# A planned attention and mixer kernel on one core: the set-up reordered, one more transpose and mixer buffer, a new plan

## The chip, the cores and the metric

The kernel runs on one core of a Trainium2 chip. The metric is the device time of one execution in microseconds. Five engines work side by side, each through its own queue in order: PE (matrix multiply), DVE (VectorE), ACT (ScalarE), POOL (GpSimd) and SP, which here only issues transfers. An instruction that waits for a semaphore holds back everything behind it on its engine.

## The reference, cut to what matters

The sequence has 2048 tokens (16 tiles of 128) of width D = 448, all in bf16. Two layers run one after the other with the same weights, each an attention block (16 heads of 28) and a mixer block:

```
_A_ref(x, wqkv, wo):  qkv = x @ wqkv;  p = softmax(q k^T / sqrt(28));  return (p v) @ wo
_B_ref(x, w1, w2, w3, w4):
    h  = gelu(layernorm(x) @ w1)
    hs = (four quarters of h, shifted by -1, +1, -2, +2 tokens) @ w2
    x1 = x + hs
    return x1 + gelu(layernorm(x1) @ w3) @ w4

x = x + _A_ref(layernorm(x), A_wqkv, A_wo)
x = x + _B_ref(layernorm(x), B_w1, B_w2, B_w3, B_w4)
(both lines once more)
```

The softmax needs some bound on each row of scores. The kernel takes a bias from norms: for each head the largest squared norm of a key, scaled by the square root of a ratio between the key weights and the query weights. That ratio only shifts the scores; the softmax does not depend on its exact value.

## The kernel before, in words

**Attention.** The heads are stored in groups of 32 columns, so that four groups `g` of four heads fill 128 partitions. The scores are formed as key tile by query chunk: a *block* is one key tile (128 keys) of one head against one query chunk of 512 (or two key tiles against a chunk of 256). ACT takes the exponential of blocks in PSUM (line 1367), three blocks in one instruction (128x1536) and two in the next (128x1024), and writes them to `PT`. PE then multiplies `PT` with the values `vaug` (line 736); column 28 of each head in `vaug` is 1.0, so that the sum of the exponentials comes out with the values. A few blocks do not go to ACT: DVE computes their exponential by a polynomial into buffers `PD` (lines 1253, 1274, 1276, 1278, 1281). There are 1024 blocks in each layer.

**Order of the blocks.** `ORDER` lists segments (query chunk, first and last key tile), each for g = 0 to 3. Layer 0 begins with query chunk 0 against key tiles 0 to 3 (64 blocks), then tiles 4 to 7 (blocks 64 to 127), then 8 to 15 (from block 128), and only then goes on to query chunk 1. Layer 1 begins with query chunk 0 against key tiles 0 to 6 (112 blocks), then query chunk 1 against the same tiles. A segment that carries on an earlier one first needs the norm bound over all its key tiles, and adds the difference to the stored queries (`t_qp`, line 1234).

**Projections.** A layer norm writes a tile to `xn`; it is transposed to `xT` (two buffers of 512 tokens), by PE for the first chunk and by a transposing transfer afterwards. From `xT` PE forms keys, values and queries (line 745, `wk_pad`, `wv`, `wq_pad`). ACT or POOL squares keys and queries; PE sums the squares per head with `astat` (keys) or `astatq` (queries), and DVE takes the largest (`kmaxc`, line 1036). A transposed buffer is held from its load until every projection from it is done.

**Set-up.** DVE and POOL write constants and pads, among them the pad columns of `vaug` (POOL, lines 804 and 805). The query and key weights are packed to 32 columns per head (lines 828 to 833). The ratio comes from the squares of all 448 weight rows (line 839), summed by PE (line 841 holds the DVE form of the square), with a square root on POOL (line 854). It goes into `RTN` (line 856), which scales the key bound, and into `astatq` (line 860), which scales the summed squares of the query. The first query chunk adds that sum into its own PSUM bank (line 1067) before it is copied out (line 1060 or 1058).

**Who decides the order.** All work is written as small tasks that yield operations with an assumed duration. When the kernel is built, a planner (`Sched`) takes the tasks in order of priority (`RANK`, `Q_LEAD`), assigns buffers and PSUM banks, and writes down one fixed order for each engine. While PE would idle, it inserts *fillers*, small matmuls on `ident` (line 1783) whose result is never read. `D_RATE` and `DPK` say how many blocks DVE may take. `DOUBT` adds time to what PE waits for when the planner compares candidates. On the chip each engine simply follows its list.

**Mixer.** `t_mixA` normalises, transposes and multiplies with `w1`; `t_mixB` does the shifted multiply with `w2` into a buffer `x1b` (two of them), normalises, transposes, and multiplies with `w3` and `w4`. It runs beside the exponentials of the next query chunks; for the last chunk of layer 1 it forms the tail of the kernel. The GELU of a group is one long ACT instruction with a table load before and after it.

Of the kernel before, what the change touches and what calls it, by code (L numbers as in the profile page):

```python
# [515 lines left out]
DPK = 1  # L516
RANK = {k: round(1.1 + 0.05 * i, 3) for i, k in enumerate([('a', 0, 0), ('k', 0, 1), ('b', 0, 0), ('b', 0, 1), ('k', 1, 0), ('k', 0, 2), ('q', 0, 1), ('k', 0, 3), ('k', 1, 1), ('k', 1, 2), ('a', 0, 1), ('q', 0, 2), ('q', 0, 3), ('a', 0, 2), ('q', 1, 0), ('q', 1, 1), ('b', 0, 3), ('b', 0, 2), ('a', 0, 3), ('a', 0, 4), ('k', 1, 3), ('b', 0, 4), ('k', 1, 4), ('b', 1, 0), ('a', 1, 3), ('a', 1, 0), ('q', 1, 3), ('a', 1, 4), ('a', 1, 2), ('a', 1, 1), ('b', 1, 4), ('q', 1, 2), ('b', 1, 3), ('b', 1, 2), ('b', 1, 1)])}
Q_LEAD = {(0, 1): 4, (0, 2): 10, (0, 3): 3, (1, 0): 9, (1, 1): 8, (1, 2): 4, (1, 3): 3}
D_RATE = {(0, 0): 0.08, (0, 1): 0.05, (0, 2): 0.05, (0, 3): 0.13, (1, 0): 0.16, (1, 1): 0.1, (1, 2): 0.16}
# [10 lines left out]
Sched.DOUBT = {"dma": 1.0, "pool": 0.4, "dve": 0.05, "act": 0.2}  # L530
# [14 lines left out]
def build_kernel(nc, A_x, A_wqkv, A_wo, B_x, B_w1, B_w2, B_w3, B_w4, out, n_layers=2):  # L545
    S = A_x.shape[1]
    D = 448
# [19 lines left out]
    NPD = 6  # L567
# [56 lines left out]
    with st:  # L624
# [15 lines left out]
        halfs = sb("halfs", [128, 4], FP32)  # L640
        neghalf = sb("neghalf", [128, 4], FP32)
# [7 lines left out]
        x1b = sb("x1b", [128, 2, D], FP32)  # L649
# [42 lines left out]
        RTN, TMP, T2 = (sc[:, i, :] for i in range(3))  # L692
# [7 lines left out]
        xst = h2T[:, :, :].rearrange("p a b -> p (a b)").rearrange("p (t d) -> p t d", d=D)  # L700

# [56 lines left out]
        def t_load():  # L758
# [3 lines left out]
            def xload(a, b, t):  # L762
                return dma("sp", lambda e: e.dma_start(out=xst[:, a:b, :], in_=xin[:, a:b, :]), writes=[(("xst",), i) for i in range(a, b)], t=t)

            yield xload(0, 1, 3.0)
            yield xload(1, 2, 3.1)
            yield xload(2, 3, 3.2)
            yield xload(3, 4, 3.3)
            for ci, d3 in ((1, wst[1]), (0, wst[0])):
                yield dma("sp", lambda e, d3=d3, ci=ci: e.dma_start(out=d3[:, 0:3, :], in_=A_wqkv[0:384, ci * D:(ci + 1) * D].rearrange("(c p) n -> p c n", p=128)),  # L770
                          writes=[("pt", 4 * ci + k) for k in range(3)], t=4.6 + 1.4 * (1 - ci))
                yield dma("sp", lambda e, d3=d3, ci=ci: e.dma_start(out=d3[0:64, 3, :], in_=A_wqkv[384:448, ci * D:(ci + 1) * D]),
                          writes=[("pt", 4 * ci + 3)], t=4.6 + 1.4 * (1 - ci))
            yield dma("sp", lambda e: e.dma_start(out=wv[:, 0:3, :], in_=A_wqkv[0:384, 2 * D:3 * D].rearrange("(c p) n -> p c n", p=128)), writes=[(("wv",), 0)], t=6.0)
            yield dma("sp", lambda e: e.dma_start(out=wv[0:64, 3, :], in_=A_wqkv[384:448, 2 * D:3 * D]), writes=[(("wv",), 1)], t=6.0)
            yield xload(4, 8, 8.0)
            yield ("wait", ("start",))
            yield xload(8, 12, 8.0)
            yield xload(12, 16, 9.0)
# [12 lines left out]
        def t_setup():  # L792
            wst = [PT[:, 0:4, 0:D], PT[:, 4:8, 0:D]]
            wsq = PT[:, 8:12, :]
            yield op("dve", 0.1, lambda e: e.memset(ones_f[:, :], 1.0), writes=[("ones_f",)])
            yield op("dve", 0.1, lambda e: e.memset(ones_bf[:, :], 1.0), writes=[("ones_bf",)])
            yield op("pool", 0.5, lambda e: e.affine_select(out=ident[:, :], in_=ones_bf[:, :], pattern=[[-1, 128]],
# [6 lines left out]
            yield op("pool", 1.3, lambda e: e.memset(vaug[:, :, :].rearrange("p t (h r) -> p t h r", r=32)[:, :, :, 28:32], 0.0), writes=[("vaug_all",)])  # L804
# [1075 lines left out]
```

## Time and profile before

| | us |
|---|---|
| three runs | 1082.04, 1082.95, 1082.1 (median 1082.1) |
| the profiled execution, its own time | 1080.76 |
| the profiled execution, span from the first to the last instruction | 1079.0 |
| busy: PE / ACT / DVE / POOL | 1009.5 / 1016.7 / 642.3 / 315.8 |
| first exponential starts | 21.83 |
| last exponential ends | 1024.65 |
| granted TensorE clock | 0.994 |

A line of the profile's groups names line, engine, operation, output and input with their shapes, the count, busy time and mean duration, and then the idle time just before these instructions and what ended most of it. In the timeline the columns are start, length, engine, line and operation; what stands in brackets is the idle time before it and the instruction that released it. The profiled execution took 1.34 us less than the median of the runs, and 1.76 us of it lie outside the span.

### The profile page before, as it was taken

The page shows a single profiled execution, that of the slowest core. Times are in us where ns is not written, and L with a number is a line of the kernel's source. Part 1 is how long each engine was busy: PE and PEld are TensorE (multiplying, and loading weights), DVE is VectorE, ACT ScalarE, POOL GpSimd, SP SyncE. Part 2 cuts the span into 40 slices and gives each one's busy share as a digit, 9 for nine tenths or more (in the row PEclk, how much of TensorE's full clock was granted, in tenths as well). Part 3 has the DMA queues.
Part 4 walks back from the last instruction along what each step waited for, and adds up shares of the span by engine and source line. Part 5 has one row for each costly group of instructions (what it writes and reads, how often), then busy time and mean ns, then how long its engine had stood idle before and what let it go on. Part 6 is the DMA issues. An engine that isn't in the chain of part 4 may idle for free.

```text
span 1079.0 us, 35560 instructions
## 1 busy us (share of the span) xinstructions
PE 1009.5 (94%) x16117; PEld 426.2 (39%) x16117; DVE 642.3 (60%) x1250; ACT 1016.7 (94%) x922; POOL 315.8 (29%) x503
## 2 busy tenths in 40 slices
PE   6999899999989999999999999999899999999998
PEld 3333343443333244333333334353333343444465
DVE  8766678846588525675446652524685685564451
ACT  5999899999999999999998999999999999999952
POOL 3244126302264014453212210102624230432140
PEclk9999999999999999999999999999999999999999
DMA  4438211003121013211121222423321110121000
GB/s 134 118 97 233 69 57 32 21 19 91 32 31 32 12 57 79 49 31 27 35 85 41 44 79 92 137 58 99 61 42 36 38 45 13 32 65 30 2 20 33
DMA packets 92615, 62.27 MB, mean 58 GB/s; under 512 B 64688, under 2 KB 82368, under 8 KB 92464
## 3 DMA queue, kind: packets, MB, share of 16 engines
q1 hardware_dynamic: 89088, 51.92, 18.9%
q0 software_dynamic: 3376, 8.09, 2.7%
q8 instruction: 126, 2.06, 0.8%
q14 instruction: 25, 0.20, 0.1%
HBM read 27.12 MB, written 15.71 MB: 40 GB/s over the span
## 4 chain that ended last, share of the span: by engine, by line
ACT 72%; PE 18%; DVE 6%; DMA 3%; issue 1%; POOL 1%; SPq 0%; DVEq 0%; ACTq 0%
ACT PT L1367 65%; PE ps L745 9%; PE ps L1212 4%; PE ps L736 4%; ACT h2T L1742 3%; ACT fb L1616 1%; DMA rT<-ub 1%; PE ps L1783 1%; ACT L1742 1%; DMA xT<-xn 1%; ACT L1367 1%; DVE st L876 1%; DMA fb<-rscr 0%; DVE rT L1461 0%; DVE hT L1596 0%
## 5 line engine op out<-in xcount | busy, mean ns | idle before, releaser
L1367 ACT ACTIVATE PT<-ps 128x1536 bf16<-128x1536 f32 (+1 forms) x803 | 918.8, 1338 | 17.6 <-PE ps L1212 16.8
L1212 PE MATMUL ps<-qT,kT 32*128 32x512 bf16 (+1 forms) x2560 | 314.7, 341 | 35.4 <-ACT PT L1367 26.7
L736 PE MATMUL ps<-PT,vaug 128*32 128x512 bf16 (+1 forms) x2520 | 250.7, 341 | 0.2 <-DVE ub L1446 0.2
L1212 PEld LDWEIGHTS ps<-qT,kT 32*128 32x128 bf16 x2560 | 80.5, 91 | 310.1 <-ACT PT L1367 279.5
L1783 PE MATMUL ps<-ident 128*32 128x256 bf16 x3860 | 173.4, 278 | 6.0 <-DVE qT L1084 2.2
L745 PE MATMUL ps<-xT,w 128*32 128x512 bf16 (+2 forms) x2176 | 165.0, 362 | 5.3 <-DMA xT<-xn 3.2
L1783 PEld LDWEIGHTS ps<-ident 128*32 128x32 bf16 x3860 | 110.7, 97 | 38.0 <-issue 13.2
L1733 DVE CAST h2T<-ps 128x512 bf16<-128x512 f32 (+2 forms) x109 | 65.7, 603 | 79.0 <-PE ps L745 70.1
L736 PEld LDWEIGHTS ps<-PT,vaug 128*32 128x32 bf16 x2520 | 74.8, 95 | 92.8 <-issue 79.3
L745 PE MATMUL ps<-w,h2T 128*32 128x448 bf16 x1512 | 100.7, 357 | 9.0 <-ACT h2T L1742 9.0
L1472 POOL TENSOR_TENSOR otn<-ub,fb 128x512 bf16<-128x512 f32 (+1 forms) x36 | 42.1, 1169 | 150.8 <-DMA fb<-rscr 150.5
L745 PEld LDWEIGHTS ps<-xT,w 128*32 128x32 bf16 (+1 forms) x2176 | 59.6, 96 | 55.5 <-issue 29.3
L1011 POOL TENSOR_TENSOR sq<-kT 128x512 bf16<-128x512 bf16 (+2 forms) x32 | 30.2, 947 | 122.7 <-DVE kT L1025 122.6
L1614 POOL TENSOR_TENSOR fb<-hT 112x512 f32<-112x512 bf16 (+1 forms) x36 | 38.6, 1074 | 71.6 <-DVE hT L1596 54.7
L745 PEld LDWEIGHTS ps<-w,h2T 128*32 128x32 bf16 x1512 | 40.7, 96 | 43.1 <-issue 14.6
L1688 POOL TENSOR_TENSOR x_res<-x_res,x1b 128x448 f32<-128x448 f32 x32 | 40.1, 1257 | 35.8 <-DVE xn L896 30.8
L745 PE MATMUL ps<-xT,wk_pad 128*32 128x512 bf16 (+2 forms) x576 | 48.8, 359 | 0.4 <-DVE qT L1058 0.4
L1461 DVE RECIPROCAL rT<-rT 16x128 f32<-16x128 f32 (+1 forms) x36 | 33.6, 934 | 22.2 <-DMA rT<-ub 22.1
L1253 DVE TENSOR_SCALAR yd<-ps 128x512 int32<-128x512 f32 x40 | 27.2, 685 | 31.4 <-PE ps L1212 30.8
L1011 POOL TENSOR_TENSOR sq<-qT 128x512 bf16<-128x512 bf16 x28 | 29.6, 1065 | 49.0 <-DVE qT L1058 44.7
L745 PE MATMUL ps<-xT,wq_pad 128*32 128x512 bf16 x512 | 42.8, 382 | 0.1
L745 PE MATMUL ps<-wv,xT 128*32 128x448 bf16 x512 | 41.2, 356 | 1.2 <-DVE kmaxc L1036 0.8
(152 smaller groups left out, 1107.9 us busy)
## 6 DMA issues: line engine op xcount, KB each, us to landing
uscr<-ub SPq DMA_DIRECT2D x24, 256.0 KB, 2.7
ub<-uscr SPq DMA_DIRECT2D x24, 256.0 KB
fb<-rscr SPq DMA_DIRECT2D x24, 256.0 KB
xnd<-xn SPq DMA_DIRECT2D x28, 128.0 KB, 1.8
x_res<-in_A_x_dram POOLq DMA_DIRECT2D x16, 224.0 KB, 3.4
xd<-x_res SPq DMA_DIRECT2D x16, 224.0 KB, 3.1
x_res<-xd SPq DMA_DIRECT2D x16, 224.0 KB, 3.6
out_dram<-obf SPq DMA_DIRECT2D x16, 112.0 KB
```

Of the source, the lines that this page charges most:

```text
L736: return lambda e: e.matmul(out=out, lhsT=lhsT, rhs=rhs, start=start, stop=stop, **kw)
L745: r.append(e.matmul(out=out[c:c + w, :], lhsT=lhsT[:, c:c + w], rhs=rhs, start=start, stop=stop, tile_position=(0, c)))
L1011: return op("pool", 0.15 + NW * 0.0018, lambda e: e.tensor_tensor(out=sq[:, si, 0:NW], in0=src, in1=src, op=ALU.mult), reads=rk, writes=[( ...
L1212: yield op("pe", max(0.055, 0.22 / nc_ * NW / 512.0), lambda e, i=i, kc=kc, j=j, g=g, a=a, NW=NW, bank=bank: e.matmul(out=ps[:, bank, i * ...
L1367: yield op("act", 0.06 + n * w * 0.000833, lambda e, bk=bk, s0=s0, n=n, w=w: e.activation(out=PT[:, s0:s0 + n, 0:w], in_=ps[:, bk[0]:bk[0] ...
L1461: yield op("dve", 0.86, lambda e: e.reciprocal(out=rT[0:4 * n, :], in_=rT[0:4 * n, :]), reads=[("rT",)], writes=[("rT",)])
L1472: yield op("pool", 0.2 + NW * 0.0021, lambda e: e.tensor_tensor(out=otn[:, g, 0:NW], in0=u, in1=rb[:, 0:NW], op=ALU.mult), reads=[uk, fk], ...
L1614: yield op("pool", 0.2 + NW * 0.00165, lambda e: e.tensor_tensor(out=f, in0=z, in1=z, op=ALU.mult), reads=hk, writes=[fk])
L1688: yield op("pool", 1.2, lambda e: e.tensor_tensor(out=X, in0=X, in1=X1, op=ALU.add), reads=[xk, ("x1b", s)], writes=[xk], deps=[nop_])
L1733: ev = op("dve", c_ps(NW), lambda e, fch=fch, b=b: e.tensor_copy(out=hb[:, fch, 0:NW], in_=ps[:, bi(b), 0:NW]), reads=[("ps", bi(b))], wri ...
L1742: yield op("act", c_act(nl * NW), lambda e: e.activation(out=hb[:, 0:nl, 0:NW], in_=hb[:, 0:nl, 0:NW], func=ACT.Gelu_apprx_tanh), reads=al ...
L1783: return [e.matmul(out=ps[32 * c:32 * c + 32, bi(b), 0:256].rearrange("p (a n) -> p a n", n=128), lhsT=ident[:, 32 * c:32 * c + 32], rhs=i ...
```

## The change

**Ratio.** The squares are taken from the first 128 weight rows only (one ACT square of 128x512 for each weight instead of two of 128x1024), so the ratio has 8 one-column matmuls on PE instead of 32. The small DVE steps are fewer. For the first query chunk the ratio is no longer in the matrix that PE uses: a constant matrix `astat0` (−0.5 in column 28) takes its place, and the copy of the queries out of PSUM multiplies by a column `rcol` that is the ratio in row 28 and 1 elsewhere.

**Pads and constants.** ACT writes the pads of `vaug` (two activations with scale 0 and with 1). `astat` comes from an indicator that POOL makes with two selects. The tasks of set-up are split, and what is not needed early is put after the first normalised tiles. The first four tiles are transposed in one PSUM bank each.

**Buffers.** After layer 0's last use, four key slots of `kT` serve as a third buffer for transposed tiles. `x1b` has three buffers. `PD` has four instead of six.

**Plan.** Priorities, leads, rates and doubts are new.

```diff
-DPK = 1
-RANK = ...
-Q_LEAD = {(0, 1): 4, (0, 2): 10, (0, 3): 3, (1, 0): 9, (1, 1): 8, (1, 2): 4, (1, 3): 3}
-D_RATE = {(0, 0): 0.08, (0, 1): 0.05, (0, 2): 0.05, (0, 3): 0.13, (1, 0): 0.16, (1, 1): 0.1, (1, 2): 0.16}
+DPK = 2
+RANK = ...
+Q_LEAD = {(0, 1): 6, (0, 2): 9, (0, 3): 3, (1, 0): 7, (1, 1): 9, (1, 2): 4, (1, 3): 5}
+D_RATE = {(0, 0): 0.08, (0, 1): 0.05, (0, 2): 0.05, (0, 3): 0.06, (1, 0): 0.16, (1, 1): 0.1, (1, 2): 0.16}
...
-Sched.DOUBT = {"dma": 1.0, "pool": 0.4, "dve": 0.05, "act": 0.2}
+Sched.DOUBT = {"dma": 0.8, "pool": 0.4, "dve": 0.05, "act": 0.05}
...
-    NPD = 6
+    NPD = 4
...
-        x1b = sb("x1b", [128, 2, D], FP32)
+        x1b = sb("x1b", [128, 3, D], FP32)
...
+        def xv(xt):
+            return xT[:, xt, :, :] if xt < 2 else kT[:, :, 128 * 9:128 * 13]
+
+        def xts():
+            return XT + (["xT2"] if ("third",) in SC.events else [])
+
+        def t_third():
+            yield ("wait", ("kvfree",))
+            yield op("pool", 0.2, lambda e: e.memset(kT[:, :, 128 * 9:128 * 9 + 1], 0.0), writes=...)
+            yield ("sig", ("third",))
...
+        def t_setup_act():
+            pads = vaug[:, :, :].rearrange("p t (h r) -> p (t h) r", r=32)
+            yield op("act", 1.4, lambda e: e.activation(out=pads[:, :, 28:32], in_=ones_bf[:, 0:4].unsqueeze(1).to_broadcast([128, 16 * NKV, 4]), func=ACT.Copy, scale=0.0), ...)
+            yield op("act", 0.45, lambda e: e.activation(out=pads[:, :, 28:29], in_=ones_bf[:, 0:1].unsqueeze(1).to_broadcast([128, 16 * NKV, 1]), func=ACT.Copy), ...)
...
+        def t_squares(i, wp, nm):
+            yield op("act", 0.48, lambda e: e.activation(out=wsqs[i], in_=wp[:, 0, :], func=ACT.Square), ...)
+            yield ("sig", ("wsq", i))
+
+        def t_ratio():
+            yield ("wait", ("astat",))
             b = yield ("acq", MISC[0:3])
-            for kind, (wp, nm) in enumerate(((wk_pad, "wk_pad"), (wq_pad, "wq_pad"))):
-                for hf in range(2):
-                    fcs = slice(2 * hf, 2 * hf + 2)
-                    yield op("act", 0.95, lambda e, wp=wp, fcs=fcs: e.activation(out=wsq[:, fcs, :], in_=wp[:, fcs, :], func=ACT.Square), ...)
+            for kind, i in enumerate((1, 0)):
+                yield ("wait", ("wsq", i))
                 for g in range(4):
-                    for fc in range(4):
-                        yield op("pe", 0.06, mm(...), ...)
+                    yield op("pe", 0.035, mm(...), ...)
...
+            yield op("dve", 0.12, lambda e: e.reciprocal(out=T2, in_=RIN), ...)
+            yield op("dve", 0.1, lambda e: e.scalar_tensor_tensor(out=rcol[:, :], in0=T2, scalar=M28, in1=no28[:, :], op0=ALU.mult, op1=ALU.add), ...)
+            yield ("sig", ("rcol",))
...
-            yield from tr_pe(slots, xt)
+                yield ("sig", ("xn1", t))
+            yield from tr_pe(slots, xt, 1)
...
-                yield ("wait", ("acol",))
-                yield op("pe", c_mm(512), lambda e: e.matmul(out=ps[:, bi(b), :], lhsT=astatq[:, g, :], rhs=sq[:, si, :], ...), ...)
+                yield ("wait", ("no28",))
+                yield op("pe", c_mm(512), lambda e: e.matmul(out=ps[:, bi(b), :], lhsT=astat0[:, :], rhs=sq[:, si, :], ...), ...)
                 yield ("rel", s)
                 yield ("wait", ("bc", L, p0, g))
-                yield evac()
+                yield ("wait", ("rcol",))
+                yield op("dve", c_ps2(512), lambda e: e.tensor_scalar(out=dst, in0=ps[:, bi(b), :], scalar1=rcol[:, g:g + 1], scalar2=bias, op0=ALU.mult, op1=ALU.add), ...,
+                         alt=[alt("act", 0.1 + c_act(512), lambda e: e.activation(out=dst, in_=ps[:, bi(b), :], func=ACT.Identity, scale=rcol[:, g:g + 1], bias=bias))])
...
-            x1s = yield ("acq", ["x10", "x11"], [k for rk in rks for k in rk])
+            x1s = yield ("acq", ["x10", "x11", "x12"], [k for rk in rks for k in rk])
...
-            x_ = yield ("acq", XT, ...)
+            x_ = yield ("acq", xts(), ...)
...
+        SC.spawn(t_third(), 3)
```

Because the planner writes the lists anew, the orders on the engines differ throughout. Counted from the two sets of lists: the blocks that DVE takes fall from 40 to 37; fillers fall from 3860 to 3688; the eight group GELUs of ACT keep their count, and the last one is 128x7168 instead of 128x5632 with three single ones before it; three copies of first values to `vaug` move from ACT to DVE; one of the four packs of the query weights moves from ACT to POOL; SP issues 324 transfers in both.

## The prediction

> **What bounds the kernel now.** I read the page first, then ACT's busy time by stretch, the timeline of the first 35 us, PE's busy time by stretch, and last the timeline around each long wait of ACT.
>
> From the page, its header and its parts 1, 4 and 5:
>
> ```profile
> span 1079.0 us, 35560 instructions
> PE 1009.5 (94%) x16117; PEld 426.2 (39%) x16117; DVE 642.3 (60%) x1250; ACT 1016.7 (94%) x922; POOL 315.8 (29%) x503
> ...
> ACT 72%; PE 18%; DVE 6%; DMA 3%; issue 1%; POOL 1%; SPq 0%; DVEq 0%; ACTq 0%
> ...
> L1367 ACT ACTIVATE PT<-ps 128x1536 bf16<-128x1536 f32 (+1 forms) x803 | 918.8, 1338 | 17.6 <-PE ps L1212 16.8
> ```
>
> ACT bounds it: 72% of the chain that ended last is ACT's, nearly all of it the exponentials of L1367. PE's 94% holds 173.4 us of fillers (L1783), so PE has room on the whole, but not everywhere. The time is therefore first exponential, plus ACT's work, plus ACT's idle time until the last one, plus the tail. ACT by stretch (length, busy, count):
>
> ```profile
> 21.80:1024.70 1002.90, 985.00 (x870) 0.99 0.23 58
> 109.00:115.00 6.00, 2.94 (x4) 0.72 0.34 104
> 339.00:344.10 5.10, 2.73 (x4) 0.67 0.01 3
> 569.00:573.30 4.30, 0.41 (x2) 1.00 0.26 83
> 741.00:785.00 44.00, 41.59 (x39) 1.00 0.30 63
> 785.00:820.10 35.10, 32.54 (x30) 0.95 0.24 43
> ```
>
> Between the first and last exponential ACT is idle for 17.9 us: about 2.0 at 30, and 3.1, 2.4, 3.9, 2.4 and 2.6 in the five stretches. The tail is 1079.0 − 1024.65 = 54.3 us. How the 21.83 us of set-up arise, from the timeline:
>
> ```profile
> 6.45 1.97 ACT L828 ACTIVATE wk_pad<-PT 128x448 bf16<-128x448 bf16 x4 [4.38 <-DMA PT<-in_A_wqkv_dram]
> ...
> 9.62 1.61 DVE L919 COPY xT<-ps 128x512 bf16<-128x512 bf16 x4
> ...
> 11.28 1.05 PE L745 MATMUL ps<-xT,wk_pad 128*32 128x512 bf16 x16
> ...
> 13.74 1.05 ACT L839 ACTIVATE PT<-wq_pad 128x1024 bf16<-128x1024 bf16 x1
> ...
> 17.78 1.01 POOL L854 TENSOR_TENSOR sc<-sc,halfs 128x4 f32<-128x4 f32 x1 [7.67 <-DVE sc L853]
> ...
> 20.65 0.69 ACT L1060 ACTIVATE qT<-ps,bc 128x512 bf16<-128x512 f32 x1 [0.43 <-DVE bc L1168]
> ...
> 21.83 2.37 ACT L1367 ACTIVATE PT<-ps 128x1536 bf16<-128x1536 f32 x2 [0.49 <-PE ps L1212]
> ```
>
> The first key norms are there at 14.96 (L1036, 14.28 + 0.68). From then on only the ratio is waited for: its last square ends at 14.79, its sums reach DVE behind layer norm statistics at 16.14, POOL's root ends at 18.79, the query copy starts at 20.65.
>
> **The change part by part. Set-up.** Durations are those of the same rows. Before, the statistics of the first four tiles run at 4.32, 5.07, 5.80 and 6.53, back to back behind DVE's constants, which end at 4.4. The new list puts ten short memsets and two small writes ahead of them, ending near 2.6 (sum of the old rows, 0.06 to 0.27 each). Then the input's landing decides: transfers carried 448 KB of x by about 3.9 us, and the key weights' last bytes, near 5.5 us, were seen by ACT at 6.45, so I add 1 us: the tiles land at about 3.4, 3.9, 4.5 and 4.9 (estimate). At the old pitch of 0.75 the last statistics end 0.9 us earlier. Copies out of PSUM by single tile, one of them on ACT, end near 9.75 instead of 11.23. PE now has the ratio's nine small matmuls ahead of the key projection, and their last input waits for POOL's first query pack (0.58, after weights landing near 7.9) and an ACT square (0.57, between the rows for 448 and 512 elements): 9.2, then PE, DVE, PE to about 10.1. So the keys start at 10.1 instead of 11.28. From there: 1.05 keys, 0.9 queries (their four packs on POOL, 4 × 0.58, end at 10.2: in time), 0.4 norm sums, 0.69 largest, 0.45 two bias steps, 0.79 query copy, 0.5 scores, and about 0.5 of semaphores: first exponential at 15.3, 6.5 us earlier. The ratio's root (1.01) ends near 12, before the bias steps want it.
>
> The query copy now has two column operands. The row with one took 0.69. [...]
>
> The pads go to ACT. On POOL they took 1.32 and 1.69 (L804, L805). The nearest ACT row is 0.49 for 128x384[...]. They lie in ACT's 4.38 us wait for the weights, after the table load ends at 2.07, and end near 4: free. [...] On DVE, at the rate of L810 (0.17 for 128x128 uint32), they would cost about 1.2 us ahead of the statistics, of which 0.8 is slack to the landing. Where the row shows ACT waiting, ACT is the better place, by 0 to 0.4 us.
>
> **What the early stage gives back.** All 16 tiles' keys must be projected before block 128. PE by stretch:
>
> ```profile
> 21.39:32.00 10.61, 9.59 (x137) 3.31 (x137) 10.49 (x30) 8.36 (x9) 1.27 (x2) 1.00 0.38 100
> ...
> 43.00:54.60 11.60, 11.38 (x151) 3.77 (x153) 9.03 (x27) 11.60 (x11) 3.61 (x3) 1.00 0.21 70
> ...
> 75.00:85.00 10.00, 10.00 (x134) 3.34 (x133) 5.77 (x13) 10.00 (x9) 9.94 (x15) 1.00 0.69 198
> ```
>
> The first pair of numbers after the length is PE's. Over 11.2 to 85.0, when 51 exponentials (128 blocks) have started, PE is idle for 5.05 us in all, and the fillers at 29 to 31 take 1.24. So 67.5 us of PE work are needed, 1.2 less without the ratio's matmuls. Keys from 10.1 make it 76.4. The new list has 112 fillers from block 15 to 135, most of them at blocks 35 to 48 where it waits for the second chunk's transpose: 3.8 us at 0.034 each. With 3.2 us of idle time, what the old kernel had after its first score, block 128 starts at 83.4 instead of 85.0. DVE tells the same: in the new list the statistics of three chunks and four value copies stand between the first scores and the second group's query copy (some 12 us of rows), and the last norm sums of chunks 1 and 3 stand right at blocks 63 and 128, with two to three 16-matmul projections (0.94 to 1.05 each) between them and the scores that need them. So ACT starts 6.5 us earlier but waits more: **−1.6 us** kept. Ends: −6.5 (no new wait) and +1 (transposes late).
>
> **Two waits that the new order takes away.** Timeline:
>
> ```profile
> 108.62 0.94 DVE L1461 RECIPROCAL rT<-rT 16x128 f32<-16x128 f32 x1 [2.75 <-DMA rT<-ub]
> ...
> 568.27 1.04 PE L745 MATMUL ps<-xT,wq_pad 128*32 128x512 bf16 x16
> ...
> 573.21 2.37 ACT L1367 ACTIVATE PT<-ps 128x1024 bf16<-128x1024 f32 x2 [3.89 <-PE ps L1212]
> ```
>
> At 108 DVE waits for a transfer of 6.3 us that runs beside the load of w3 and w4. Behind it in DVE's queue stands the last query add of chunk 1 (L1084), PE waits for that, ACT for PE: 2.5 us. In the new list all four of these adds and one more copy stand ahead of the reciprocal; behind it stands one add for chunk 2, wanted far later. **−2.5**; ends 0 and −3.1.
>
> At 569 layer 1 goes over to query chunk 1. The old list projects these queries exactly there (after 1392 score matmuls, where they are needed), the new one after 1337 to 1352, some 16 exponentials or 20 us earlier. **−3.6** of 3.89; ends 0 and −3.9.
>
> **ACT's work.** Three more blocks on ACT. 62 exponentials took 70.17 us, so a block takes 70.17/155 = 0.453: **+1.4**. DVE loses three chains of four operations, which it has room for. The ACT squares and value copies that go lie before the first exponential; those behind it are as many as before.
>
> **Tail.** ACT is busy from the last exponential for 13.2 us either way (table load 1.28, GELUs 1.85 + 4.89 before, 6.18 after, eleven short GELUs and four of 0.42). Then PE is full. The third `x1b` removes the split of the w2 matmuls (32 at 1037.84, 16 at 1044.14) and the wait of about 1 us before 1050.8; 40 w3 matmuls (0.054 each) have moved ahead of the end, under cover, and 24 more fillers stand there: **−0.6**; ends −2.2 and +0.5.
>
> **The rest.** SP issues as many transfers; the third transpose buffer's memset on POOL (0.1) hangs on nothing near. The waits at 339, 741 to 770 and 816 (7.4 us) come from late DVE or transposing transfers beside a list that expects them sooner; nothing in the new lists lets me say which go. 0, ends ±3.
>
> Sum: −1.6 − 2.5 − 3.6 + 1.4 − 0.6 = −6.9. Against the profiled 1080.8 that is 1073.9; against the median of 1082.1, 1.3 above it, **1075.2**.
>
> **The rivals.** *The whole early start is kept.* If the waits at blocks 15, 63 and 128 fall within ACT's two buffered units, the first term is −6.5: 1082.1 − 11.8 = 1070.3. For it: ACT has 2.26 us of scores ahead. Against it: PE's stretches are full.
>
> *The plan's new waits eat it.* Waits of the kind at 339 and 816 arise wherever a list is written from assumed durations; with the doubt for transfers cut from 1.0 to 0.8, PE commits earlier to late data. With 4 to 6 us of new ones: 1079 to 1082, centre 1080.
>
> *Slower, by one mechanism: the transposes of chunks 1 and 3 land late.* Their key projections stand on PE directly before blocks 64 and 128. Each transposing load stands on SP behind five or four stores of normalised tiles, which wait for DVE. A landing later than the list expects stops PE, scores and ACT one for one. It decides once both together lose 9.1 us more than my sum has (6.9 + 2.2). Old loads landed 4.3 us after issue; they would have to double. Price at that point: 1084.3 and more.
>
> *It doesn't do what it says:* if the key pack or x lands later than I think, the ratio is not the last thing any more and the start gains less; that is inside the first rival's other end.
>
> **How the numbers follow.** A measurement of this kernel tells about 0.2% (2.2 us) from no change: faster is below 1079.9, slower above 1084.3. Likeliest case 0.53 (its own range 1072 to 1078.5), whole start kept 0.20, eaten 0.22 (half of it below 1079.9), slower 0.05. Faster 0.53 + 0.20 + 0.11 = 0.84; same 0.11; slower 0.05. The range reaches from 1070.0 to 1081.0.
>
> **What would show it.** First exponential at 15 to 16; ACT waits of 2 to 4 us near blocks 15, 63 and 128; block 128 near 83; no wait of over 1 us after the first reciprocal and none at the change to query chunk 1 in layer 1; exponentials of about 920 us in all; a tail near 53.7. Wrong if the start is not before 17, if block 128 comes before 80 or after 86, or if new waits of ACT past block 128 come to over 4 us.

## The result and the profile after

The kernel after takes 1077.68 us (median of four runs, 1076.24 to 1079.42), the kernel before 1082.37 on the same chip: a ratio of 0.9957, interval 0.994 to 0.9974. The forecast was 1075.2, in a range of 1070.0 to 1081.0. The profiled execution of after took 1079.42 us, the slowest of its four; forecast for the profiled pair was 1073.9. From the page of after, the lines that answer to those shown of before:

```profile
span 1077.7 us, 35124 instructions
PE 1006.0 (93%) x15918; PEld 420.7 (39%) x15921; DVE 637.4 (59%) x1234; ACT 1017.9 (94%) x919; POOL 312.7 (29%) x506
...
ACT 73%; PE 17%; DVE 6%; DMA 2%; issue 1%; POOL 1%; SPq 0%; DVEq 0%
...
L1447 ACT ACTIVATE PT<-ps 128x1536 bf16<-128x1536 f32 (+1 forms) x805 | 921.7, 1336 | 17.9 <-PE ps L1292 17.1
```

L1447 is L1367 of before, L1292 is L1212. The sum of ACT's idle time is the same as before (17.9 against 17.6 us), but it lies elsewhere. ACT by stretch, first before, then after (length, busy, count, granted clock):

```profile
21.80:84.90 63.10, 60.67 (x57) 1.00 0.42 119
84.90:1024.70 939.80, 924.33 (x814) 0.99 0.21 53
```

```profile
17.20:87.85 70.65, 61.08 (x58) 1.00 0.47 125
87.85:1022.40 934.55, 925.61 (x815) 0.99 0.21 53
90.00:120.00 30.00, 30.00 (x29) 1.00 0.53 157
535.00:575.00 40.00, 39.87 (x38) 1.00 0.36 87
```

Both cuts stand at the 52nd exponential, where block 128 begins. Up to there before is idle for 2.43 us and after for 9.57; from there on 15.47 and 8.94. The waits at 109 and at 569 are gone: ACT has no gap between 90 and 120 and 0.13 us between 535 and 575. In after DVE still stands for the first reciprocal's transfer, but only one query add is left behind it, and the queries of layer 1's chunk 1, which before projects from 566 us on, are projected from 543 us on. The two lines, of DVE and of PE, in after:

```profile
110.91 0.94 DVE L1541 RECIPROCAL rT<-rT 16x128 f32<-16x128 f32 x1 [2.73 <-DMA rT<-ub]
...
543.08 1.25 PE L762 MATMUL ps<-kT,wq_pad 128*32 128x512 bf16 x16
```

The new waits stand in the timeline of ACT, after:

```profile
17.23 6.88 ACT L1447 ACTIVATE PT<-ps 128x1536 bf16<-128x1536 f32 x6
...
27.22 2.36 ACT L1447 ACTIVATE PT<-ps 128x1536 bf16<-128x1536 f32 x2 [1.89 <-PE ps L1292]
...
54.44 11.41 ACT L1447 ACTIVATE PT<-ps 128x1024 bf16<-128x1024 f32 x10 [3.96 <-PE ps L1292]
...
87.87 7.80 ACT L1447 ACTIVATE PT<-ps 128x1024 bf16<-128x1024 f32 x7 [3.58 <-PE ps L1292]
```

They come at blocks 15, 64 and 128. The sum of the profiled pair against the forecast (us; cuts rounded to 0.05):

| term | forecast | measured | from |
|---|---|---|---|
| start of block 128 | −1.6 | +2.95 | 84.90 to 87.85 |
| waits at 109 and 569 | −6.1 | −6.3 | 2.51 + 3.89 to 0.13 |
| other waits past block 128 | 0 ± 3 | −0.3 | 9.07 to 8.81 |
| ACT's work past block 128 | +1.4 | +1.3 | 924.33 to 925.61 |
| tail | −0.6 | +1.0 | 54.3 to 55.3 |
| span | −6.9 | −1.3 | 1079.0 to 1077.7 |

So all terms past the early stage and before the tail are right to 0.3 us, and the early stage alone is off by 4.5. The spans of the profiled pair differ by only 1.3 us, a fifth of the 6.9 forecast; the medians differ by 4.7. The profiled execution of before was 1.6 us faster than its median here, that of after 1.7 slower; the last section tells what is known of such differences.

### The profile page after: what moved, and what is told of

The parts are those of the page before. It is cut to its first block, busy times and chain, and to the rows that moved or that the text cites. A ratio compares the mean times of both kernels' runs of the same rounds, so it can differ in the third digit from the quotient of the medians.

```text
span 1077.7 us, 35124 instructions
## 1 busy us (share of the span) xinstructions
PE 1006.0 (93%) x15918; PEld 420.7 (39%) x15921; DVE 637.4 (59%) x1234; ACT 1017.9 (94%) x919; POOL 312.7 (29%) x506
## 3 DMA queue, kind: packets, MB, share of 16 engines
q8 instruction: 125, 2.05, 0.8%
## 4 chain that ended last, share of the span: by engine, by line
ACT 73%; PE 17%; DVE 6%; DMA 2%; issue 1%; POOL 1%; SPq 0%; DVEq 0%
ACT PT L1447 66%; PE ps L762 10%; PE ps L1292 4%; ACT h2T L1822 4%; PE ps L753 3%; ACT fb L1696 1%; ACT L1822 1%; DMA rT<-ub 1%; ACT L1447 1%; DVE fb L1356 1%; DVE rT L1541 0%; DVE yd L1333 0%; DVE PD L1361 0%; DVE fb L1354 0%; DMA PT<-in_A_wqkv_dram 0%
## 5 line engine op out<-in xcount | busy, mean ns | idle before, releaser
L1447 ACT ACTIVATE PT<-ps 128x1536 bf16<-128x1536 f32 (+1 forms) x805 | 921.7, 1336 | 17.9 <-PE ps L1292 17.1
L1292 PE MATMUL ps<-qT,kT 32*128 32x512 bf16 (+1 forms) x2560 | 315.2, 340 | 33.2 <-ACT PT L1447 24.0
L1292 PEld LDWEIGHTS ps<-qT,kT 32*128 32x128 bf16 x2560 | 80.7, 91 | 309.5 <-ACT PT L1447 279.9
L1863 PE MATMUL ps<-ident 128*32 128x256 bf16 x3688 | 165.3, 274 | 3.7 <-POOL ident L842 1.5
L762 PE MATMUL ps<-xT,w 128*32 128x512 bf16 (+2 forms) x1600 | 127.7, 360 | 2.6 <-DVE h2T L1813 1.6
L1863 PEld LDWEIGHTS ps<-ident 128*32 128x32 bf16 x3688 | 105.0, 96 | 31.0 <-issue 11.9
L762 PE MATMUL ps<-w,h2T 128*32 128x448 bf16 x1512 | 103.1, 360 | 10.2 <-ACT h2T L1822 9.8
L1552 POOL TENSOR_TENSOR otn<-ub,fb 128x512 bf16<-128x512 f32 (+1 forms) x36 | 40.3, 1119 | 175.6 <-DMA fb<-rscr 172.5
L762 PEld LDWEIGHTS ps<-xT,w 128*32 128x32 bf16 (+1 forms) x1600 | 44.2, 95 | 41.8 <-issue 19.3
L762 PE MATMUL ps<-kT,w 128*32 128x512 bf16 (+2 forms) x576 | 40.0, 360 | 2.5 <-DVE qT L1164 1.4
L1822 ACT ACTIVATE h2T<-h2T 128x7168 bf16<-128x7168 bf16 (+2 forms) x8 | 42.0, 5244 | 0.1
L1526 DVE COPY ub<-ps 128x512 f32<-128x512 f32 (+1 forms) x40 | 23.3, 582 | 30.7 <-PE ps L753 30.1
L762 PE MATMUL ps<-xT,wq_pad 128*32 128x512 bf16 x448 | 40.2, 396 | 0.6 <-DVE kmaxc L1113 0.3
```

The costliest lines, as they stand in the source:

```text
L762: r.append(e.matmul(out=out[c:c + w, :], lhsT=lhsT[:, c:c + w], rhs=rhs, start=start, stop=stop, tile_position=(0, c)))
L1292: yield op("pe", max(0.055, 0.22 / nc_ * NW / 512.0), lambda e, i=i, kc=kc, j=j, g=g, a=a, NW=NW, bank=bank: e.matmul(out=ps[:, bank, i * ...
L1447: yield op("act", 0.06 + n * w * 0.000833, lambda e, bk=bk, s0=s0, n=n, w=w: e.activation(out=PT[:, s0:s0 + n, 0:w], in_=ps[:, bk[0]:bk[0] ...
L1552: yield op("pool", 0.2 + NW * 0.0021, lambda e: e.tensor_tensor(out=otn[:, g, 0:NW], in0=u, in1=rb[:, 0:NW], op=ALU.mult), reads=[uk, fk], ...
L1822: yield op("act", c_act(nl * NW), lambda e: e.activation(out=hb[:, 0:nl, 0:NW], in_=hb[:, 0:nl, 0:NW], func=ACT.Gelu_apprx_tanh), reads=al ...
L1863: return [e.matmul(out=ps[32 * c:32 * c + 32, bi(b), 0:256].rearrange("p (a n) -> p a n", n=128), lhsT=ident[:, 32 * c:32 * c + 32], rhs=i ...
```

## The experiments

Two kinds of edit were used. In one, the planner runs again. In the other, the written lists are kept and single instructions are put in or moved: `put(engine, fn, deps, mark)` puts one ahead of `mark`. A ratio is to the kernel before, run on the same chip in the same session.

**Does the early start count? A delay.**

```diff
 # after, lists kept
+put("act", lambda e: e.activation(out=w4[:, 0:11, :]..., in_=ones_bf[:, 0:1].to_broadcast([128, 4928]), func=ACT.Copy), ..., first exponential)
```

> The kernel after with its written order kept, and one more ScalarE copy (128x4928 of ones into a weight buffer that is loaded much later) directly ahead of the first exponential: about 4.3 us of ScalarE work, so the first exponential starts near 21.5 instead of 17.2. Theory 1 (the stage up to block 128 is paced by the key projections and what follows them on TensorE and VectorE, not by ScalarE's start): the waits of ScalarE at 27, 54 and 88 (1.9, 4.0, 3.6 us) shrink by most of this, block 128 starts within 1.5 us of 87.9, and the whole grows by 0 to 1.5 us. Theory 2 (each us of an earlier start counts at the end): the waits stay, block 128 starts near 92, and the whole grows by about 4.3 us.

Measured: 1.0022 (1.0 to 1.0044), 1084.87 us. A kernel of the same session that keeps after's timing from 17 us on (`e2_warm`, next) had 0.9948, so 4.3 us of work cost 7.5 between the medians. The timeline of this kernel is that of a second set of runs.

> The kernel of e1_delay again, for its trace at the full clock. Theory (a later start is passed on because ScalarE's own list holds the key squares behind exponentials and TensorE's list holds scores, which wait for exponentials, ahead of projections): first exponential near 21.6, the waits near 31, 59 and 92 as long as in the kernel after (1.9, 4.0, 3.6 us), block 128 near 92. Rival (the early stage is elastic): these waits 4 us shorter in sum, block 128 near 88.

Measured: 1.002 (0.9996 to 1.0044), 1083.15 us. ACT's timeline of this kernel:

```profile
17.32 4.30 ACT L1923 ACTIVATE w<-ones_bf 128x4928 bf16<-128x4928 bf16 x1
21.52 3.70 ACT L1447 ACTIVATE PT<-ps 128x1536 bf16<-128x1536 f32 x3
...
30.59 0.60 ACT L1085 ACTIVATE sq<-ps 128x512 bf16<-128x512 f32 x1 [0.34 <-PE ps L762]
...
34.00 2.36 ACT L1447 ACTIVATE PT<-ps 128x1536 bf16<-128x1536 f32 x2 [1.89 <-PE ps L1292]
...
61.22 11.41 ACT L1447 ACTIVATE PT<-ps 128x1024 bf16<-128x1024 f32 x10 [3.96 <-PE ps L1292]
...
94.65 5.54 ACT L1447 ACTIVATE PT<-ps 128x1024 bf16<-128x1024 f32 x5 [3.58 <-PE ps L1292]
```

The waits did not take up the delay: 1.89, 3.96 and 3.58 us are exactly those of after, and block 128 starts at 94.65, 6.8 us later, where the theory said 92. Theory 1 of e1_delay falls, and so does the rival of an elastic stage. The early stage is not a fixed amount of PE work beside which ACT may start sooner or later. The written lists tie both: ACT squares keys of the first chunk (L1085, 30.59) behind exponentials, and PE's scores, which wait for exponentials, stand ahead of projections. The 2.5 us beyond the delay arise before the wait at 34: PE is idle for 4.8 of the 10 us from 15 to 25, while ACT copies, and the granted clock is 0.68 from 20 to 25 and 0.64 from 25 to 30. After that wait the distance to after stays at 6.8. So within one list a shift of the start is passed on whole. What took the gain away in after are the waits that its new list itself contains.

**Why was PE slow at the start? Fillers.** In after PE runs the first key and query projections at half the speed of before (1.05 and 1.04 us there):

```profile
10.11 1.90 PE L762 MATMUL ps<-xT,wk_pad 128*32 128x512 bf16 x16
...
11.79 1.92 PE L762 MATMUL ps<-xT,wq_pad 128*32 128x512 bf16 x16
```

```diff
 # after, lists kept: 64 filler matmuls
+for _ in range(16): put("pe", filler, ..., first transpose)
```

> The kernel after with its written order kept, and 64 filler matmuls on TensorE (16 groups of four, of 128x256) ahead of the first transpose, where TensorE waits for 4 us. Theory 1 on the speed: TensorE ran the first key and query projections at half speed (1.90 and 1.92 us) because it had worked too little before them; with the fillers they take 1.05 each and the first exponential starts near 15.5 instead of 17.2. Rival: the half speed has another cause[...], and they stay at 1.9. On the time: if the start does not set block 128, the whole changes by less than 0.8 us; if it does, it falls by 1.7 us.

Measured: 0.9948 (0.9928 to 0.9969). The timeline of PE and PE by stretch (the last number but two is the granted clock):

```profile
1.52 3.64 PE L1863 MATMUL ps<-ident 128*32 128x256 bf16 x68 [1.52 <-POOL ident L842]
...
10.33 1.90 PE L762 MATMUL ps<-xT,wk_pad 128*32 128x512 bf16 x16
```

```profile
8.00:10.00 2.00, 1.14 (x16) 0.63 (x13) 1.18 (x7) 2.00 (x5) 1.91 (x4) 0.56 1.07 290
10.00:12.00 2.00, 1.79 (x17) 0.72 (x21) 1.33 (x8) 0.11 (x1) 0.82 (x2) 0.50 1.07 335
```

The fillers sped up the transposes (8 of them in 0.70 us instead of 1.04), but from 5 to 10 us PE worked for only 2.53, and the projections were slow again, 1.90, as the rival had said. But no further cause is needed: the record shows a granted clock of 0.50 there. The fillers stood too early. The next kernel puts some directly ahead of the keys; the unchanged kernel after ran beside it.

> The kernel after, unchanged, on the chip of the next three, to compare them with it. Expected: the same as at first, 0.9957 of the kernel before within 0.002.

Measured: 0.9967 (0.9951 to 0.9983), 1077.91 us.

```diff
 # after, lists kept: 84 + 12 + 4 + 4 + 4 filler matmuls
+for mark, n in ((first transpose, 21), (first ratio matmul, 3), (fifth, 1), (ninth, 1), (first key projection, 1)):
+    for _ in range(n): put("pe", filler, ..., mark)
```

> The kernel after with its written order kept, and 108 filler matmuls ahead of the first key projection: 84 ahead of the first transposes, and 12 + 4 + 4 + 4 between the second transposes, the ratio's small matmuls and the key projection, so that TensorE has no long pause from 1.5 us on. Theory (its speed follows how busy it was in the last microseconds): the key and query projections take 1.05 us each instead of 1.90, the first exponential starts near 15.6; and since the earlier delay of the start was passed on to the end in full, the time falls by 1.5 to 2 us. Rival 1 (the half speed has another cause): 1.90 again, no change. Rival 2 (block 128 is bound by later work alone): the start comes earlier, block 128 stays at 87.9, the time within 0.5 us.

Measured: 0.996 (0.9943 to 0.9976), 1076.82 us. PE's timeline and ACT's first exponentials:

```profile
10.97 1.04 PE L762 MATMUL ps<-xT,wk_pad 128*32 128x512 bf16 x16
11.83 1.04 PE L762 MATMUL ps<-xT,wq_pad 128*32 128x512 bf16 x16
```

```profile
16.32 4.62 ACT L1447 ACTIVATE PT<-ps 128x1536 bf16<-128x1536 f32 x4
```

Here the speed followed how busy PE had been: it worked for 3.85 us of 5 to 10 where it works for 2.95 in after, and both projections are back at 1.04 us from 1.90 and 1.92. The start gains only 0.9 us and not 1.6, since POOL's first query pack came later in this execution (ACT's square of it began at 9.54 instead of 8.78) and the keys started at 10.97 instead of 10.11. Block 128 starts at 86.97, also 0.9 us earlier, as the delay made one expect. The medians say −1.1 us where 1.5 to 2 was expected, and their intervals overlap.

**Is it the reciprocal? The wait at 109 in before.**

```diff
 # before, lists kept: DVE's list
-L1461 Reciprocal rT<-rT
 L1084 TensorTensor qT<-qT,ps
 L1058 TensorScalarPtr qT<-ps,bc
+L1461 Reciprocal rT<-rT
```

> The kernel before with its written order kept, except that the first reciprocal of row sums (1007th of the list) stands two VectorE instructions later, behind the last query add of chunk 1. Theory 1 (the wait at 109 is VectorE standing at this reciprocal for a transfer, with the add behind it): ScalarE's 2.5 us of idle time near 109 to 115 go, and the whole falls by 2 to 2.5 us. Theory 2 (TensorE is late there for another reason, or the wait is given back by the next one): the whole stays within 0.8 us of the kernel before.

Measured: 0.9952 (0.9933 to 0.997), 1077.85 us. One instruction moved by two places in before gains as much as the whole change, and more than the 2 to 2.5 us expected. ACT in the page of e4_recip, idle for 14.0 us instead of 17.6, and PE and DVE by stretch in before and then in e4_recip:

```profile
L1367 ACT ACTIVATE PT<-ps 128x1536 bf16<-128x1536 f32 (+1 forms) x803 | 918.4, 1339 | 14.0 <-PE ps L1212 13.3
```

```profile
106.00:108.00 2.00, 1.66 (x18) 0.43 (x16) 0.00 (x0) 2.00 (x3) 0.00 (x0) 1.00 1.02 338
108.00:110.00 2.00, 0.00 (x0) 0.00 (x0) 1.38 (x2) 1.27 (x2) 0.00 (x0) 1.00 0.99 331
110.00:112.00 2.00, 1.83 (x26) 0.85 (x30) 0.76 (x2) 0.21 (x1) 1.04 (x1) 0.56 0.09 25
112.00:114.00 2.00, 2.00 (x31) 0.81 (x27) 0.05 (x1) 1.74 (x2) 0.00 (x0) 0.59 0.09 19
```

```profile
108.00:110.00 2.00, 2.00 (x41) 1.06 (x37) 0.94 (x1) 2.00 (x3) 1.04 (x1) 1.00 1.03 342
110.00:112.00 2.00, 1.97 (x36) 0.73 (x29) 0.69 (x1) 2.00 (x3) 0.00 (x0) 1.00 0.18 57
112.00:114.00 2.00, 1.95 (x43) 1.08 (x41) 0.41 (x1) 2.00 (x3) 0.00 (x0) 1.00 0.07 12
```

The columns after the length are PE, its weight loads, DVE, ACT and POOL, each busy time with its count, and then the granted clock. In before, DVE stands 2.75 us for the transfer with the query add behind it, PE is empty from 108 to 110, and then the granted clock is 0.56 and 0.59 for 4 us: PE works without a pause, but at half speed for about 3.4 us (2 × 2 × 0.44 + 2 × 2 × 0.41). In e4_recip there is no pause, and the clock stays at 1.00. So what ACT waits here has two parts, a pause of 2.17 us on PE and the half speed that follows it, which also makes the next two waits (0.26 and 0.29 us behind the 2.51). The forecast's mechanism is shown; the half speed was not in it, and the whole gain (3.5 us between the spans of the profiled executions) is larger than the 2.5 it named.

Not every pause of this length had this effect: see the last section.

**Is it the third buffer? The wait at 569.**

```diff
-        SC.spawn(t_third(), 3)
```

> The kernel after without the third transpose buffer (its memset and its use left out; all else is planned again, and up to the end of layer 0's last chunk the order is the same). Theory 1 (the third buffer lets the queries of layer 1's chunk 1 be loaded and projected early): the wait of 3 to 4 us near 569 comes back, and the whole grows by 2 to 4 us. Theory 2 (the new leads and ranks do it): no wait of over 1 us there, the whole within 1 us of the kernel after.

Measured: 1.0085 (1.0068 to 1.0102), 1091.57 us, 14 us above after. Neither theory: there is no wait near 569, so the new leads and ranks are enough for that, but the whole is far slower. From ACT's timeline:

```profile
696.92 3.71 ACT L1447 ACTIVATE PT<-ps 128x1536 bf16<-128x1536 f32 x3 [4.70 <-PE ps L1292]
...
1067.30 0.60 ACT L986 ACTIVATE xT<-ps 128x512 bf16<-128x512 bf16 x1 [13.03 <-PE ps L978]
```

With two buffers a long GELU stands at 1030 us, ahead of the last two exponentials, and ACT waits for the last transposes until 1067. What the new numbers do with the third buffer lies there and at 697, not at 569.

**Set-up and buffers without the new numbers.**

```diff
 # after, planned again with the numbers of before
-DPK, RANK, Q_LEAD, D_RATE, DOUBT of after
+DPK, RANK, Q_LEAD, D_RATE, DOUBT of before
```

> The kernel after (new set-up, third transpose and mixer buffers) with the old numbers of the plan (DPK 1, the old ranks, leads, rates and doubts). Theory (the order of set-up gives its 4.6 us at the start back by block 128, and the gain comes from where the new numbers put the later work): no gain, the time at or above the kernel before (1081 to 1090 us), with waits of several us past block 128. Rival (the set-up and the buffers carry the gain): 1076 to 1079 us.

Measured: 1.0038 (1.0019 to 1.0058), 1086.88 us. Shown: with the old numbers the new set-up and buffers gain nothing. ACT's waits there are 0.9 us at 51, 1.7 at 68 and 4.3 at block 128, 3.0 at 113 to 116 (the reciprocal's place again), 3.1 at 697 and 3.7 at 822; none at 569. So each of the two, new numbers with two buffers and old numbers with three, is free of that wait, and both are slower than after. It looks as if a plan's numbers fit one set of buffers; two plans don't show it.

**Block 64: the normalisations chunk after chunk.** In after, chunk 1's tiles are normalised between those of chunks 2 and 3, and its transposing load is issued at 35.40 instead of 27.00.

```diff
             if c > 1:
                 yield ("wait", ("start",))
+                yield ("wait", ("xnd", 0, 4 * c - 1))
...
-            yield from xload(4, 8, 8.0)
+            yield from xload(4, 8, 5.0)
```

> The kernel after with layer 0's first normalisations done chunk after chunk (chunk 2 waits for the last store of chunk 1, chunk 3 for that of chunk 2) and with the load of x for chunk 1 assumed to land after 5 us instead of 8; planned again. Theory (block 64 waits because chunk 1's normalised tiles stand on VectorE between those of chunks 2 and 3, so that its transpose is issued at 35 us): the transpose is issued before 28, the wait of 4.0 us at block 64 goes, the one at block 128 becomes 2 to 4 us, block 128 starts near 85, and the time falls by 2 to 3 us. Rival (the wait moves to block 15 or 128 in full, since TensorE has no room): block 128 stays within 0.7 of 87.9 and the time within 0.7 us.

Measured: 1.0007 (0.9992 to 1.0021), 1082.52 us, slower than after. ACT's timeline, and PE by stretch:

```profile
54.08 1.02 ACT L1448 ACTIVATE PT<-ps 128x1024 bf16<-128x1024 f32 x1 [1.14 <-PE ps L1293]
...
86.81 10.06 ACT L1448 ACTIVATE PT<-ps 128x1024 bf16<-128x1024 f32 x9 [2.50 <-PE ps L1293]
...
112.70 2.53 ACT L1448 ACTIVATE PT<-ps 128x1536 bf16<-128x1536 f32 x2 [1.92 <-PE ps L1293]
116.37 4.62 ACT L1448 ACTIVATE PT<-ps 128x1536 bf16<-128x1536 f32 x4 [1.14 <-PE ps L1293]
```

```profile
110.00:112.00 2.00, 0.07 (x4) 0.10 (x4) 1.70 (x3) 0.78 (x1) 0.00 (x0) 1.00 0.85 280
112.00:114.00 2.00, 2.00 (x22) 0.72 (x21) 1.06 (x2) 1.30 (x1) 0.00 (x0) 0.71 0.03 5
114.00:116.00 2.00, 2.00 (x33) 1.06 (x31) 0.00 (x0) 1.17 (x2) 0.00 (x0) 0.50 0.34 104
```

The load is issued at 31.97, not before 28, and the wait at block 64 falls from 3.96 to 1.14, in part as the theory says. But block 128 gains only 1.1 us, and in the new order three query adds stand behind the first reciprocal: the wait at 109, which after had lost, is back with its pause and its clock of 0.5. The rival was nearer.

**The first group's keys first.** Before blocks 64 and 128 stands one chain: the sums of squared keys of head group 0, their largest, three small bias steps, the difference, the query shift, scores. In after its steps on DVE and PE stand between value copies and value projections.

```diff
-                yield ("spawn", k_proj(L, c, g, xt), RANK["k", L, c])
+                yield ("spawn", k_proj(L, c, g, xt), 0.9 if L == 0 and g == 0 else RANK["k", L, c])
 # and in the lists: the fillers of e5_warm2; the first reciprocal five DVE instructions later
```

> The kernel after, planned again with one rank changed: in layer 0 the key projection of the first head group of each key chunk goes ahead of everything else (0.9), so that its sums, its largest norm and the query shift that blocks 64 and 128 wait for come sooner. Besides, the 108 early fillers of e5_warm2 and the first reciprocal of row sums five VectorE instructions later, with its two transfers and its product. Theory (the waits at 54 and 88 are this chain standing behind value projections and copies): the wait of 4.0 us at block 64 falls below 1 us, block 128 starts at 83 to 85 instead of 87.9, no wait near 109 to 117, and the time falls by 2 to 4 us below the kernel after. Rival (TensorE has no room before block 128, so the wait only moves): block 128 within 1 us of 87, the time within 1 us of the kernel after.

Measured: 0.9941 (0.992 to 0.9962), 1075.46 us. The row of the page and ACT's timeline:

```profile
L1447 ACT ACTIVATE PT<-ps 128x1536 bf16<-128x1536 f32 (+1 forms) x805 | 920.4, 1338 | 12.3 <-PE ps L1292 9.4 <-PE ps L753 2.2
```

```profile
35.11 28.43 ACT L1447 ACTIVATE PT<-ps 128x1024 bf16<-128x1024 f32 x25
...
67.21 31.78 ACT L1447 ACTIVATE PT<-ps 128x1536 bf16<-128x1536 f32 x28 [2.21 <-PE ps L753]
```

From 35 to 63 us ACT has no gap, so the wait at block 64 is gone; in its place come 1.25 us at 64.8 and 2.21 us at 67.21. The 14th of the 28 at 67.21 is the 52nd exponential and starts near 82.0: block 128 is 5.9 us earlier than in after, with nothing waiting there, nor near 109 (1.14 us stand at 120). Of the 5.9, 1.6 are the earlier first exponential (15.60), and about 4.1 the waits at blocks 64 and 128, 7.54 us in after and 3.46 here. The profiled execution has a span of 1070.0. It is the fastest of all kernels by its median of six runs, but its interval overlaps that of after (0.9951 to 0.9983 in the second session, on another chip), so that it beats after is likely, not shown. Three things were changed at once, and the lists were planned again; what each is worth at the end was not separated.

> As e8_keys_first, and in addition the first normalisations of layer 0 chunk after chunk. Theory: chunk 1's transpose is issued before 28 us, and block 128 comes 1 to 2 us earlier still than in e8_keys_first, the time 1 to 2 us lower. Rival (as e6_seq showed, an order that is better on paper lets TensorE pause elsewhere, and the pause is followed by some 3.4 us at half clock): block 128 earlier, but new waits with a granted clock of 0.5 to 0.8 beside them, the time at or above that of the kernel after.

Measured: 0.9978 (0.9963 to 0.9992), 1080.13 us. Chunk 1's load is issued at 28.40, and the rival is right in the main: PE pauses from 50 to 52 (0.06 us busy), the clock is 0.50 from 54 to 56, and ACT waits 1.7 and 1.3 us there. Block 128 starts near 84.5, later than in e8_keys_first and not earlier. The step that looks better alone makes the whole slower, for the second time.

**A second reciprocal.** In e8_keys_first the same pattern stands at 730 us in layer 1.

```diff
 # e8_keys_first, lists kept: DVE's list
-L1541 Reciprocal rT<-rT
 L1164 TensorTensor qT<-qT,ps
 L1135 TensorScalarPtr qT<-ps,bc
 L1164 TensorTensor qT<-qT,ps
+L1541 Reciprocal rT<-rT
```

> As e8_keys_first, with one more reciprocal of row sums moved: in layer 1 the one that waited 3.46 us for its transfer at 730 us stands three VectorE instructions later, behind two query adds and a query copy. Theory (same pattern as at 109: VectorE stands for the transfer, TensorE for VectorE, and the pause is followed by about 3.4 us at half clock): the wait of 2.6 us near 735 and the drop of the granted clock to 0.56 at 732 to 736 go, the time falls by 1.5 to 2.6 us below e8_keys_first. Rival (the wait there is TensorE's own load): a wait of over 1.5 us stays near 735, the time within 0.7 us of e8_keys_first.

Measured: 0.9955 (0.9938 to 0.9972), 1076.53 us: no gain over e8_keys_first. ACT's timeline, and PE by stretch:

```profile
744.01 1.02 ACT L1447 ACTIVATE PT<-ps 128x1024 bf16<-128x1024 f32 x1 [1.26 <-PE ps L1292]
746.56 3.87 ACT L1447 ACTIVATE PT<-ps 128x1536 bf16<-128x1536 f32 x3 [1.53 <-PE ps L1292]
```

```profile
742.00:744.00 2.00, 1.12 (x10) 0.31 (x14) 1.09 (x2) 0.75 (x1) 0.82 (x1) 0.73 0.03 10
744.00:746.00 2.00, 2.00 (x21) 0.65 (x21) 0.17 (x1) 1.02 (x1) 0.00 (x0) 0.50 0.38 125
```

The wait at 735 is gone, but one of 1.26 + 1.53 us stands ten us later: PE now pauses 1.41 us for a normalised value (`otn`, L1552; its product on POOL starts at 741.56, in e8_keys_first at 737.87), and the clock falls to 0.50 there. At 109 the products had slack; here they seem to have none. Neither theory is right as written.

## Why the forecast was right, and where its steps were wrong

**Right:** the sign and, between the medians and within 2.5 us, the size. That size is in part luck: the terms measured on the profiled pair come to −1.3 and not −6.9, and what brings the medians to −4.7 is no term of the forecast. The waits at 109 and 569 were named with place, cause and size, and both are gone (−6.3 for −6.1). For 109 the cause is shown by e4_recip. For 569 the measured fact is that the queries are projected some 23 us earlier; which number of the plan does it was not separated, and e7_oldplan shows that old numbers with a third buffer do it too. ACT's work past block 128 (+1.3 for +1.4) is right. The rest (−0.3 in a band of ±3) is luck: the waits at 339 to 344 and 812 to 820 fell from 4.9 to 1.3 us, which the forecast said it could not tell, and about 4.6 us of new ones stand at 155, 455 to 459, 528, 632, 787 to 790 and 885. The query copy with two columns took 0.78 (0.79 forecast, the author's estimate beside the 0.69 of the row with one), and the key projection started at 10.11 (10.1 forecast).

**Wrong: the early stage, −1.6 forecast, +2.95 measured.** The forecast's own signs of being wrong came true: the first exponential starts at 17.23 (15.3 forecast, wrong if not before 17), block 128 at 87.87 (wrong if after 86), and the new waits past it make more than 4 us. Two terms of the early stage's sum were mis-sized. PE's work from the first key projection to block 128 was forecast as 67.5 − 1.2 + 3.8 = 70.1 us and measured as 71.39; the two projections at half speed are 1.7 of it. Their durations were taken from the row of before, where 24 fillers stand around and after the transposes; after has 8 there. e5_warm2 shows that the missing work is the cause of the half speed (1.04 us with its fillers, 1.90 and 1.92 without); it is worth 0.9 us at block 128 in an execution in which the keys came 0.86 us later. The same 1.7 us are most of what the first exponential is late. PE's idle time was forecast as 3.2 us and measured as 6.37 (77.76 − 71.39). This is the larger error. The forecast saw the chain with its projections in between "right at blocks 63 and 128", but then it took the idle time of before for after. e8_keys_first shows what the chain was worth: put ahead, it takes about 4.1 us off the waits. And PE's amount of work does not set block 128 alone, as the sum had it: in e1_delay_again the projections are the same, and the later start of ACT moves block 128 by more than its own length.

**Wrong, but of no effect: the pads.** The second one, 128x368 single elements 32 apart, took 1.80 us on ACT, where the plan assumed 0.45 and the row of before for 128x384 has 0.49; the first took 1.43 (1.4 assumed). They end at 5.35, where near 4 was the author's estimate, and still before the key weights at 6.09.

**Wrong: the tail, −0.6 forecast, +1.0 measured.** PE is idle for 4.68 us of the tail (55.35 − 50.67) instead of 3.39; ACT waits 2.48 us there at 1039 where before waits 1.85 and 0.40. No experiment was made on it.

**The rivals.** "The plan's new waits eat it" is half right: the new waits are there, 7.1 us more in the early stage, and they are not the work of the changed doubt: e7_oldplan, with the old one, waits 6.9 us at 51, 68 and 87. Past block 128, where the rival put them, about 4.6 us of new ones came as well, but as much of the old ones went. The slower case (late transposes) may have come in part: chunk 1's load was issued at 35.40, and with an issue at 31.97 block 64 waits 2.8 us less (e6_seq). But in e8_keys_first block 64 does not wait at all with an issue at 33.8, so the load is not its only cause. The early stage lost 4.5 us more than forecast, where 9.1 would have decided.

## What to carry to other kernels

A gain at the start of a kernel is worth what is left of it at the next fixed point; find that point, and size its idle time from the new order, not from the old trace. An instruction that waits for a transfer is placed behind those that feed the next engine, as far as its own results have slack. And a pause on PE is priced with the half clock that can follow it: a stall of about 2 us in this kernel took another 3.4 us of slow work with it in some places (2.17 us ahead of 110 in before) and none in others (1.97 ahead of 388 in before).

## What the runs showed of the hardware that was not expected

- Pauses of PE of 1.4 to 2.4 us were followed by about 3.4 us at half clock, in before at 110 (a pause of 2.17 us), in e6_seq at 112 (2.42), in e8_keys_first at 732 (1.50) and in e10_two_recips at 743 (1.41). But most pauses of this length were not: of the twelve of 1.41 to 2.20 us past the set-up in before and after, seven left the clock at 1.00, and in e8_keys_first the clock stayed at 1.00 from 115 to 125, with PE idle for 2.05 us of the first five. One pause of 2.20 us, ahead of the matmuls that follow a long GELU, was followed by half clock in after; in after_again, where it stands 0.8 us earlier, the clock is 1.00 from 515 to 530. PE in after and then in after_again, and two stretches of after:

```profile
523.94 4.04 PE L762 MATMUL ps<-w,h2T 128*32 128x448 bf16 x48 [2.20 <-ACT h2T L1822]
...
523.15 2.45 PE L762 MATMUL ps<-w,h2T 128*32 128x448 bf16 x48 [2.20 <-ACT h2T L1822]
```

```profile
520.38:523.79 3.41, 1.36 (x42) 0.98 (x34) 0.62 (x1) 3.41 (x1) 0.00 (x0) 1.00 0.00 0
523.79:527.20 3.41, 3.26 (x36) 1.41 (x40) 0.00 (x0) 3.38 (x4) 0.00 (x0) 0.50 0.02 5
```

- Why the clock fell after this pause in one execution and not in the other is not shown. In the records of before and after, the changes of the clock stand at multiples of 3.41 us from one another (in after the stretches between them are 440.32, 3.41, 64.85, 3.41, 256.00, 3.41 and 290.13 us). With the span cut at these multiples, past the set-up the two traces have four stretches of 3.41 us at full clock in which PE was busy for at most 0.41 of the time (0.29 and 0.41 in before from 106.82 and 932.85, 0.40 and 0.15 in after from 520.38 and 1073.34), and each was followed by half clock. Of the ten with 0.45 to 0.63, four were (0.58 and 0.48 in before from 335.51 and 813.38, 0.63 and 0.53 in after from 452.11 and 779.79) and six were not, so in these two traces the busy share alone does not tell them apart.
- In after the granted clock reads 1.00 from 10 to 14 us, but the projections there take 1.90 and 1.92 us. The first entry of its record, to full clock, stands at 15.20; in before it stands at 11.25, ahead of projections of 1.05 and 1.04. In after_again, which also reads 1.00 there, they take 1.90 and 1.62. In e2_warm the record shows 0.50 from 10 to 14 us, and they take 1.90 and 1.92.
- The time of a run follows its mean granted clock: over 48 runs of the kernel before on one chip it rose by 0.74 us for each 0.001 that the clock was lower. One stretch of 3.41 us at half clock lowers the mean by 0.0016 (1.71 of 1079 us), so by this slope it costs an estimated 1.2 us. The kernel after had a mean clock of 0.9949 over 14 runs, before 0.9933 over 58 beside it; by that slope 1.2 us of the 4.1 between their medians come with it, one such stretch fewer. Why the medians of the first session differ by 3.4 us more than the spans of the profiled pair is not shown beyond this. Two executions of one kernel can differ as much: the profiled one of after_again is 5.1 us longer than that of after, with seven such stretches among the exponentials instead of three, and 2.5 us of waits at 992 to 997, where the clock is 0.50 (990 to 995) and 0.87 (995 to 1000), that the first one did not have.
